# Cosine attention with a mixture of adapters on one core: sums of k and v of the last two batches kept head by head, and one tile multiplied in quarters of the array

## The chip, the cores and the metric

The kernel runs on one core of a Trainium2 chip. The metric is the time of one execution on the device, in microseconds (us). TensorE (PE; its weight loads are shown as PEld) multiplies matrices into PSUM. VectorE (DVE), ScalarE (ACT) and GpSimd (POOL) work element by element. SyncE (SP) and GpSimd issue the transfers (DMA) between HBM and the on-chip memory SBUF. Each engine runs its own list of instructions in order, and semaphores tell one engine that another has finished something.

## The reference

Linear attention with cosine weights over 8 batches of 8 heads, 576 positions and 64 dimensions, and then a mixture of eight low-rank adapters, two of them chosen for each of the 4608 rows:

```python
def phi(x, c, s):
    r = np.maximum(x, 0.0)
    return np.concatenate([r * c, r * s], axis=-1)
q_p, k_p = phi(q, cos_w, sin_w), phi(k, cos_w, sin_w)
kv = np.einsum('bhsf,bhsd->bhfd', k_p, v)
z = np.sum(k_p, axis=2)
num = np.einsum('bhsf,bhfd->bhsd', q_p, kv)
den = np.einsum('bhsf,bhf->bhs', q_p, z)[..., None] + 1e-06
x = (num / den).transpose(0, 2, 1, 3).reshape(B * S, H * D)
# then, with the two largest of the logits x @ w_gate for each row, w their softmax:
out = x + sum over the two e of  w_e * ((x @ A[e]) @ B[e])
```

## The kernel before

All matrix work is in bf16, with sums in PSUM. A table of text, `ORDER`, lists 791 steps, each with its engine letter (T TensorE, A ScalarE, V VectorE, G and W GpSimd, S SyncE) and its numbers; each engine's instructions stand in the order in which its steps stand there. There are two loops in it, interleaved: over the eight batches b, and over the 36 row tiles n of 128 rows (64 positions r times two values of s, of nine; every ninth tile, n = 4, 13, 22, 31, is mixed: one half of its rows is of one batch, the other of the next).

Steps of a batch: `ldv`, `ldk`, `ldq` load v, k and q (GpSimd issues, after the first batch). `vs` multiplies a ninth of v by a cosine or a sine; there are 18 for a batch, shared between ScalarE, GpSimd and in the first batches VectorE. `rk` and `qc` are the relu of k (one step) and of q (two steps), on VectorE (lines 251 and 282). `kv` (three parts, line 258) multiplies k and v into the PSUM tile `big`, in quarters of the array, heads by pairs. `kve` (line 275) copies that sum out of `big` into the SBUF tile `kvsb`, in bf16. `kvsb` has room for two heads side by side in its columns: the sums of heads with the first index half, g2 = 0, stand on partitions 0 to 63 in columns 0 to 64, those of g2 = 1 on partitions 64 to 127 in columns 65 to 129, with zeros elsewhere (written once by `kz`). So `kve` is two copies of 64 partitions, both on ScalarE, and the zeros let one matmul over all 128 rows give two heads without mixing them.

Steps of a tile: `qt` turns q on TensorE, `qe` multiplies it by the cosine and sine tables (VectorE, line 297, tile `qT`). `nd` multiplies it by `kvsb` into the PSUM tile `nd`, numerators and denominators together, after small matmuls that put the eps there. It has three forms: two heads at once with all 128 rows (tiles before 27); head by head with 64 rows (`by_rows`, from tile 27 on, lines 306 and 313); and for mixed tiles matmuls of 128 rows into 64 columns of the array for one batch and the other (lines 319 and 324). `re` (line 333) and `no` (lines 338 and 343) divide on VectorE and write the tile `xt`. `xt` turns it on TensorE, `xe` copies it (line 353), `za` (line 358) multiplies by the adapters' A and the gate. For groups of up to three tiles `mx`, `nm`, `mk`, `tt`, `cb`, `sg`, `zg`, `zt`, `ze` choose two adapters and weigh them. `dx` (lines 439 and 440) adds the tile and the adapters' part in a bank of `big`, which it shares with `kv`, `oe` copies it out (line 444), `st` stores it.

A step with the letter W is GpSimd's too, but waits besides for the latest VectorE step among `vs`, `rk`, `qc` that stands above it in the table. The program says so by a dependency that it calls "port".

## Time and profile before

| | |
|---|---|
| median of 3 runs | 106.73 us (106.12 to 106.85) |
| profiled execution | 105.92 us, span of the program 104.1 us |
| granted TensorE clock | 0.997 of full speed (2.4 GHz) |
| busy, TensorE / VectorE / ScalarE / GpSimd | 91.0 / 87.3 / 82.3 / 57.3 us |
| moved by DMA | 25.55 MB, mean 245 GB/s |

The span is counted from the first instruction of the program to the end of the last; the execution's time has some 1.8 us around it. Two stretches have a form of their own: up to about 26 us the first batches wait for their loads, and behind 94 us the last group's chain and the last stores run out. Between them the engines work all the time, each at its own list. An engine's busy time says how much of a stretch it worked; the chain of waits, followed back from the last instruction, names at each step who was waited for; the timeline gives each instruction with its start and its length.

### The profile page before, as it was taken

How to read it: one execution, taken by the hardware profiler on the slowest of the kernel's cores; microseconds unless marked ns; L12 is line 12 of the kernel's file. 1: busy time of each engine (PE TensorE's matmuls, PEld its weight loads, DVE VectorE, ACT ScalarE, POOL GpSimd, SP SyncE). 2: the span in 40 equal slices, each digit the busy share in tenths (PEclk: the TensorE clock that was granted, in tenths of full speed). 3: DMA queues.
4: the chain of work that ended last, by engine and by line, in shares of the span. 5: the costliest groups of instructions: out<-in, count | busy, mean ns of one | idle time of the engine just before them, and what ended most of it. 6: DMA issues, size and time to landing. Idle time of an engine off the chain costs nothing.

```text
span 104.1 us, 3984 instructions
## 1 busy us (share of the span) xinstructions
PE 91.0 (87%) x1620; PEld 65.7 (63%) x1620; DVE 87.3 (84%) x264; ACT 82.3 (79%) x176; POOL 57.3 (55%) x112
## 2 busy tenths in 40 slices
PE   4999489879794999999999999999999999998810
PEld 1344267457573887867887789688778677665200
DVE  5058769579995999999999999999999999999710
ACT  6969767918899699999899789979984896967820
POOL 6991004960799696997979869998910000000000
PEclk9999999999999999999999999999999999999998
DMA  2999999999999999999999999999999996989992
GB/s 27 364 358 291 216 208 247 208 207 213 203 208 213 204 206 210 208 213 204 208 210 205 208 207 207 210 206 126 188 397 372 349 334 257 376 307 383 381 384 96
DMA packets 19225, 25.55 MB, mean 245 GB/s; under 512 B 2184, under 2 KB 13448, under 8 KB 19208
## 3 DMA queue, kind: packets, MB, share of 16 engines
q0 software_dynamic: 11616, 12.98, 73.8%
q1 hardware_dynamic: 7064, 12.21, 32.8%
q8 instruction: 12, 0.20, 0.7%
q10 hardware_dynamic: 528, 0.13, 0.6%
q14 instruction: 5, 0.04, 0.1%
HBM read 28.85 MB, written 9.44 MB: 368 GB/s over the span
## 4 chain that ended last, share of the span: by engine, by line
PE 53%; DMA 18%; ACT 11%; POOL 9%; issue 2%; DVE 2%; POOLq 0%; ACTq 0%
DMA q<-in_q_dram 18%; PE nd L324 10%; PE big L258 8%; PE xz L349 6%; PE za L358 6%; PE big L439 6%; PE big L440 5%; PE pq L289 5%; POOL vs L244 4%; ACT xT L353 3%; ACT zgT L423 2%; PE nd L313 2%; POOL q L200 2%; PE xz L415 2%; POOL k L200 1%
## 5 line engine op out<-in xcount | busy, mean ns | idle before, releaser
L244 POOL TENSOR_SCALAR vs<-v,tab 128x256 bf16<-128x256 bf16 x78 | 37.9, 501 | 17.8 <-DMA v<-in_v_dram 8.7
L353 ACT COPY xT<-xz 128x512 bf16<-128x512 bf16 x34 | 20.0, 587 | 8.9 <-PE xz L349 8.3
L297 DVE TENSOR_TENSOR qT<-pq,tabq 128x1024 bf16<-128x1024 bf16 x36 | 23.8, 676 | 0.9 <-PE pq L289 0.8
L243 ACT ACTIVATE vs<-v,tab 128x256 bf16<-128x256 bf16 x43 | 20.0, 512 | 0.9 <-DMA v<-in_v_dram 0.6
L343 DVE TENSOR_TENSOR xt<-nd,rden 128x512 bf16<-128x512 f32 x28 | 19.2, 687 | 0.3
L324 PE MATMUL nd<-kvsb,qT 128*128 128x130 bf16 (+1 forms) x256 | 19.1, 221 | 0.4 <-DVE qT L297 0.4
L258 PE MATMUL big<-vs,k 64*64 64x130 bf16 x576 | 12.4, 221 | 4.3 <-DVE k L251 2.7
L324 PEld LDWEIGHTS <-qT 128*128 128x128 bf16 (+1 forms) x256 | 13.6, 100 | 2.9 <-issue 1.1
L349 PE MATMUL xz<-ident,xt 128*128 128x128 bf16 x144 | 14.1, 220 | 1.2 <-DVE xt L343 0.7
L358 PE MATMUL za<-AW,xT 128*128 128x136 bf16 x144 | 14.4, 223 | 0.1
L258 PEld LDWEIGHTS <-k 64*64 64x64 bf16 x576 | 9.2, 106 | 7.2 <-DVE k L251 3.5
L289 PE MATMUL pq<-ident,qq 128*128 128x128 bf16 x144 | 13.0, 219 | 0.2 <-DVE qq L282 0.2
L439 PE MATMUL big<-xt,turn 128*128 128x512 bf16 x31 | 11.7, 378 | 0.4 <-ACT k L444 0.3
L349 PEld LDWEIGHTS <-xt 128*128 128x128 bf16 x144 | 10.2, 114 | 2.6 <-DVE xt L343 0.9
L440 PE MATMUL big<-Ball,zgT 128*128 128x512 bf16 x31 | 11.8, 380 | 0.0
L468 PE MATMUL nd<-ones 128*128 128x512 bf16 x36 | 9.4, 427 | 1.5 <-DVE eps_hi L469 1.5
L275 ACT CAST kvsb<-big 64x520 bf16<-64x520 f32 x16 | 9.5, 593 | 1.5 <-PE big L258 1.1
L358 PEld LDWEIGHTS <-xT 128*128 128x128 bf16 x144 | 9.4, 98 | 1.9 <-ACT xT L353 0.8
L289 PEld LDWEIGHTS <-qq 128*128 128x128 bf16 x144 | 9.2, 98 | 1.9 <-DVE qq L282 0.3
L319 PE MATMUL nd<-eps_hi,ones 128*128 128x4 bf16 x56 | 9.5, 169 | 0.1
L282 DVE TENSOR_SCALAR qq<-q 128x1152 bf16<-128x1152 bf16 x16 | 8.1, 513 | 0.8 <-DMA q<-in_q_dram 0.8
L468 PEld LDWEIGHTS <-ones 128*128 128x128 bf16 x36 | 3.8, 108 | 6.6 <-issue 1.9
(81 smaller groups left out, 148.1 us busy)
## 6 DMA issues: line engine op xcount, KB each, us to landing
q<-in_q_dram POOLq DMA_DIRECT2D x8, 576.0 KB, 17.1
v<-in_v_dram POOLq DMA_DIRECT2D x7, 576.0 KB, 17.6
k<-in_k_dram POOLq DMA_DIRECT2D x7, 576.0 KB, 17.0
out_dram<-k SPq DMA_DIRECT2D x10, 256.0 KB, 4.2
out_dram<-v0f SPq DMA_DIRECT2D x8, 256.0 KB, 4.5
out_dram<-k0f SPq DMA_DIRECT2D x8, 256.0 KB, 3.8
out_dram<-v SPq DMA_DIRECT2D x6, 256.0 KB, 3.3
v0f<-in_v_dram SPq DMA_DIRECT2D x1, 1152.0 KB, 5.5
```

What stands on the lines that cost most here:

```text
L243: return e.activation(dst, src, AF.Copy, bias=0.0, scale=t)
L244: return e.tensor_scalar(out=dst, in0=src, scalar1=t, scalar2=1.0, op0=ALU.mult, op1=ALU.mult)
L258: e.matmul(out=big[halves[g2], par, gp * 2 * W:(gp + 1) * 2 * W], lhsT=k_b[b][pr, 2 * gp + g2, s, :], rhs=vs_t[b % NV][pr, s, 2 * gp + g2, ...
L289: e.transpose(out=d[:, gp, :, jj, :], in_=q2_t[b % 3][:, gp, s].rearrange("p g d -> p (g d)"), identity=ident)
L297: e.tensor_tensor(out=qT_t[n % NQ], in0=src, in1=tab, op=ALU.mult)
L324: e.matmul(out=nd[pr, par, gp * 2 * W:(gp + 1) * 2 * W], lhsT=qT[:, i, gp * 2 + par, js], rhs=kv_t[b % 3][:, par, gp, i, :], start=False, ...
L343: e.tensor_tensor(out=x.rearrange("p (a t d) -> p t a d", t=2, d=D), in0=nds()[:, :, :, 0:D], in1=rd.rearrange("p (t a) -> p t a", t=2).to ...
L349: e.transpose(out=xz[:, c * 128:(c + 1) * 128], in_=x[:, c], identity=ident)
L353: (e.copy if e is nc.scalar else e.tensor_copy)(xT_t[n % 3], src)
L358: e.matmul(out=zs[:, i, :], lhsT=xT_t[n % 3][:, c, :], rhs=AW[:, c, :], start=(c == 0 and i == 0), stop=(c == DCH - 1), skip_group_check=True)
L439: e.matmul(out=d, lhsT=turn, rhs=x_t[n % NX], start=True, stop=False)
L440: e.matmul(out=d, lhsT=zgT_t[g % 3][:, n - GROUPS[g][0], :], rhs=Ball, start=False, stop=True)
```

## The change

The sums of batches 6 and 7 (`dense(b)`) are no longer spread in `kvsb`: both halves go into columns 0 to 64, each on its own partitions, in one copy of 128 partitions by 520. The tiles from 27 on read them there; for `by_rows` tiles that is another column offset and nothing else. The mixed tile 31 has to be head by head then: 4 eps and 32 matmuls of 64 x 64 with 65 columns, in four quarters of the array, instead of 2 eps and 16 of 128 x 64 with 130 columns. Its division writes the same tile from another place in PSUM (`no`). `nm` gets a form for GpSimd.

```diff
-ROWS = 27
+ROWS, DENSE = 27, True
+def dense(b):
+    return DENSE and b >= ROWS // 9 * 2
     def kve(e, b, g2):
+        copy = e.copy if e is nc.scalar else e.tensor_copy
+        if dense(b):
+            return copy(kv_t[b % 3][:, :, :, :, 0:W], big[:, :, 0:4 * W].rearrange("p t (y i w) -> p t y i w", y=2, i=2))
...
     def nd_(e, n):
         qT, tok = qT_t[n % NQ], tokens(n)
+        if mixed(n) and dense(tok[0][0]):
+            jobs = [(g2, pr, js, kv_t[tok[j][0] % 3]) for g2, pr in enumerate(halves) for j, js in enumerate(halves)]
+            for g2, pr, js, _ in jobs:
+                e.matmul(out=nd[js, g2, D:4 * W:W], lhsT=ones[pr, 0:HALF], rhs=eps_hi2[pr], start=True,
+                         stop=False, skip_group_check=True)
+            for gp in range(2):
+                for par in range(2):
+                    for i in range(2):
+                        for g2, pr, js, kvb in jobs:
+                            a = gp * 2 + par
+                            e.matmul(out=nd[js, g2, a * W:(a + 1) * W], lhsT=qT[pr, i, a, js],
+                                     rhs=kvb[pr, par, gp, i, 0:W],
+                                     start=False, stop=(i == 1), skip_group_check=True)
+            return
         if by_rows(n):
-            kvb = kv_t[tok[0][0] % 3]
+            kvb, c = kv_t[tok[0][0] % 3], (0, 0 if dense(tok[0][0]) else W)
...
-                                     rhs=kvb[pr, par, gp, i, g2 * W:(g2 + 1) * W],
+                                     rhs=kvb[pr, par, gp, i, c[g2]:c[g2] + W],
...
     def no(e, n):
-        if by_rows(n):
+        if by_rows(n) or dense(tokens(n)[0][0]):
...
     def nm(e, g):
+        if e is nc.gpsimd:
+            m8 = m8_t[g % 2]
+            return e.tensor_tensor(out=ms_t[g % 2][:, 0:n], in0=m8[:, 0:n, 0], in1=m8[:, 0:n, 1], op=ALU.add)
...
-vs,G,4,5,0 vs,A,4,0,0 mx,V,10 mx,V,9 mx,V,11 nd,T,13 vs,G,4,3,0 nm,V,3 oe,A,6 rk,V,4,0 vs,W,4,2,1 oe,A,5 xt,T,12
+vs,A,4,3,1 dx,T,6,b1 vs,G,4,3,0 vs,A,4,0,0 mx,V,10 mx,V,9 mx,V,11 nd,T,13 vs,G,4,2,1 nm,V,3 oe,A,6 rk,V,4,0
+vs,W,4,1,1 oe,A,5 xt,T,12 qt,T,16 mk,V,3 re,V,13 qt,T,15 xe,A,12 tt,V,3 vs,G,4,7,0 no,V,13 dx,T,7,b1 vs,A,4,0,1
```

The table is written anew. The lists of TensorE, VectorE and SyncE have the same steps in the same order, `nm` still on VectorE. ScalarE's list loses `kve,A,6,1` and `kve,A,7,1`. GpSimd's list has the same steps in the same order too, but seven of its waits for VectorE stand one step later in the list (six letters W move, one step keeps its W and gets the next wait).

ScalarE at the sums of batch 6, before (`kvsb0` is the tile of the sums, `zgT0` the turned weights of a group, `vs1` v of batch 7):

```order
L353 COPY xT1_105<-xz_150 128x512 [waits PE_49,Activation_49]
L275 CAST kvsb0_88<-big_152 64x8x65 [waits PE_49]
L275 CAST kvsb0_88<-big_152 64x8x65
L423 COPY zgT0_120<-xz_150 128x3x2x64 [waits PE_49]
L243 ACTIVATE vs1_87<-v7_85,tab1_133 128x4x64
```

and of the change:

```order
L376 COPY xT1_105<-xz_150 128x512 [waits PE_49,Activation_49]
L279 CAST kvsb0_88<-big_152 128x8x65 [waits PE_49]
L449 COPY zgT0_120<-xz_150 128x3x2x64 [waits PE_49]
L248 ACTIVATE vs1_87<-v7_85,tab1_133 128x4x64
L248 ACTIVATE vs1_87<-v7_85,tab0_132 128x4x64
```

One copy of 128 partitions stands where two of 64 stood; the rest is as before.

GpSimd in batch 4, up to the load of q of batch 6 (`q1`), before (`vs0` is the scaled v; "waits DVE" is the wait of a W step, here for the relu of k of batch 4):

```order
L244 TENSOR_SCALAR vs0_86<-v4_82,tab0_132 128x4x64
L244 TENSOR_SCALAR vs0_86<-v4_82,tab1_133 128x4x64 [waits DVE_49]
L244 TENSOR_SCALAR vs0_86<-v4_82,tab1_133 128x4x64 [waits Pool_49]
L244 TENSOR_SCALAR vs0_86<-v4_82,tab0_132 128x4x64
L244 TENSOR_SCALAR vs0_86<-v4_82,tab1_133 128x4x64
L244 TENSOR_SCALAR vs0_86<-v4_82,tab0_132 128x4x64 x2
L244 TENSOR_SCALAR vs0_86<-v4_82,tab1_133 128x4x64 x2
L200 DMA q1_64<-in_q_dram 128x4x576 [waits DMASW3_49]
```

and of the change:

```order
L249 TENSOR_SCALAR vs0_86<-v4_82,tab0_132 128x4x64
L249 TENSOR_SCALAR vs0_86<-v4_82,tab1_133 128x4x64
L249 TENSOR_SCALAR vs0_86<-v4_82,tab1_133 128x4x64 [waits DVE_49,Pool_49]
L249 TENSOR_SCALAR vs0_86<-v4_82,tab0_132 128x4x64
L249 TENSOR_SCALAR vs0_86<-v4_82,tab1_133 128x4x64
L249 TENSOR_SCALAR vs0_86<-v4_82,tab0_132 128x4x64 x2
L249 TENSOR_SCALAR vs0_86<-v4_82,tab1_133 128x4x64 x2
L205 DMA q1_64<-in_q_dram 128x4x576 [waits DMASW3_49]
```

The wait for VectorE has gone one operation down.

GpSimd behind the load of k of batch 7 (`k7`), where the W steps of batch 5 and 6 wait for the relu of k and the second relu of q of batch 5, before:

```order
L200 DMA k7_78<-in_k_dram 128x4x576 [waits DMASW4_49]
L244 TENSOR_SCALAR vs1_87<-v5_83,tab0_132 128x4x64 [waits DVE_49,PE_49,Pool_49]
L244 TENSOR_SCALAR vs1_87<-v5_83,tab1_133 128x4x64 [waits DVE_49]
L244 TENSOR_SCALAR vs0_86<-v6_84,tab1_133 128x4x64 [waits DMASW0_49,PE_49,Pool_49]
L244 TENSOR_SCALAR vs0_86<-v6_84,tab1_133 128x4x64 [waits PE_49,Pool_49]
```

and of the change:

```order
L205 DMA k7_78<-in_k_dram 128x4x576 [waits DMASW4_49]
L249 TENSOR_SCALAR vs1_87<-v5_83,tab0_132 128x4x64 [waits PE_49,Pool_49]
L249 TENSOR_SCALAR vs1_87<-v5_83,tab1_133 128x4x64 [waits DVE_49]
L249 TENSOR_SCALAR vs0_86<-v6_84,tab1_133 128x4x64 [waits DVE_49,DMASW0_49,PE_49,Pool_49]
L249 TENSOR_SCALAR vs0_86<-v6_84,tab1_133 128x4x64 [waits PE_49,Pool_49]
```

Here the first operation behind the load has lost its wait for VectorE; the second waits for what the first waited for, and the third for what the second waited for. The other four are of the same kind: the waits for the two relus of batch 6's q, which stand behind the load of batch 7's q, and those for the relu of k of batches 6 and 7.

## Rows read from the trace of the kernel before

**Rows 1.** The page, part 1: busy us (share of the span) xinstructions.
```profile
PE 91.0 (87%) x1620; PEld 65.7 (63%) x1620; DVE 87.3 (84%) x264; ACT 82.3 (79%) x176; POOL 57.3 (55%) x112
```

**Rows 2.** Chain of waits, in order of time: start us, us, what.
```profile
70.91 0.49 ACT kvsb L275
71.42 0.59 ACT kvsb L275
```

**Rows 3.** Stretches: us, then busy us (xinstructions) by engine, clock, DMA share, GB/s.
```profile
70.00:78.00 8.00, 7.87 (x156) 6.25 (x153) 8.00 (x24) 7.36 (x17) 5.49 (x10) 1.00 1.05 234
78.00:86.00 8.00, 8.00 (x188) 5.97 (x181) 7.92 (x24) 5.92 (x12) 0.00 (x0) 1.00 0.96 353
86.00:94.00 8.00, 7.92 (x142) 5.55 (x142) 7.48 (x28) 6.00 (x13) 0.00 (x0) 1.00 0.85 315
```

**Rows 4.** Groups by line and form: busy us, mean ns of one, idle before.
```profile
L353 ACT COPY xT<-xz 128x512 bf16<-128x512 bf16 x34 | 20.0, 587 | 8.9 <-PE xz L349 8.3
...
L275 ACT CAST kvsb<-big 64x520 bf16<-64x520 f32 x16 | 9.5, 593 | 1.5 <-PE big L258 1.1
```

**Rows 5.** Timeline of weight loads at kv, batch 7: start us, us, what [idle before].
```profile
77.20 0.40 PEld L258 LDWEIGHTS <-k 64*64 64x64 bf16 x24 [0.27 <-issue]
```

**Rows 6.** Timeline of TensorE, 79 to 86 us: start us, us, what.
```profile
79.05 0.54 PE L258 MATMUL big<-vs,k 64*64 64x130 bf16 x24
79.52 0.18 PE L306 MATMUL nd<-eps_hi,ones 64*128 64x4 bf16 x2
...
79.90 0.41 PE L358 MATMUL za<-AW,xT 128*128 128x136 bf16 x4
...
83.00 0.38 PE L440 MATMUL big<-Ball,zgT 128*128 128x512 bf16 x1
83.31 0.18 PE L306 MATMUL nd<-eps_hi,ones 64*128 64x4 bf16 x2
...
84.76 0.38 PE L440 MATMUL big<-Ball,zgT 128*128 128x512 bf16 x1
84.98 0.17 PE L319 MATMUL nd<-eps_hi,ones 128*128 128x4 bf16 x1
...
85.90 0.41 PE L358 MATMUL za<-AW,xT 128*128 128x136 bf16 x4
```

**Rows 7.** Timeline of VectorE around tile 31.
```profile
84.72 1.27 DVE L297 TENSOR_TENSOR qT<-pq,tabq 128x1024 bf16<-128x1024 bf16 x2
86.01 0.21 DVE L333 RECIPROCAL rden<-nd 128x8 f32<-128x8 f32 x1
...
87.62 0.21 DVE L333 RECIPROCAL rden<-nd 128x8 f32<-128x8 f32 x1
```

**Rows 8.** Timelines of VectorE and of GpSimd at relus of k (lines 251, 244).
```profile
46.89 0.93 DVE L251 TENSOR_SCALAR k<-k 128x2304 bf16<-128x2304 bf16 x1
...
59.78 0.74 DVE L251 TENSOR_SCALAR k<-k 128x2304 bf16<-128x2304 bf16 x1
...
73.28 0.96 DVE L251 TENSOR_SCALAR k<-k 128x2304 bf16<-128x2304 bf16 x1
...
47.91 0.48 POOL L244 TENSOR_SCALAR vs<-v,tab 128x256 bf16<-128x256 bf16 x1 [0.71 <-DVE mk L380]
...
73.60 0.97 POOL L244 TENSOR_SCALAR vs<-v,tab 128x256 bf16<-128x256 bf16 x1
```

**Rows 9.** Timelines of VectorE and of GpSimd at relus of q (lines 282, 200).
```profile
51.46 0.45 DVE L282 TENSOR_SCALAR qq<-q 128x1152 bf16<-128x1152 bf16 x1
...
52.00 0.55 DVE L282 TENSOR_SCALAR qq<-q 128x1152 bf16<-128x1152 bf16 x1
...
70.17 0.79 DVE L282 TENSOR_SCALAR qq<-q 128x1152 bf16<-128x1152 bf16 x1
...
51.50 0.79 POOL L200 DMA_DIRECT2D q<-in_q_dram  x1
...
69.91 0.79 POOL L200 DMA_DIRECT2D q<-in_q_dram  x1
```

More of the change, by code (lines that the diff above doesn't have):

```diff
@@ L38 @@
+vs,G,2,4,0 qt,T,8 rk,V,2,0 nd,T,6 oe,A,0 ldq,G,4,0 xt,T,5 oe,A,1 qe,V,8 za,T,4 vs,W,2,1,1 xe,A,5 re,V,6
+vs,G,2,3,1 mx,V,4 vs,A,2,3,0 kv,T,2,0 no,V,6 ldv,G,5,0 vs,A,2,7,1 za,T,5 qc,V,2,1 vs,A,2,4,1 nd,T,7 mx,V,5
+qc,V,2,0 vs,A,2,8,1 xt,T,6 mk,V,1 kv,T,2,1 nm,V,1 re,V,7 xe,A,6 tt,V,1 cb,V,1 no,V,7 kv,T,2,2 sg,A,1 qt,T,9
 zg,V,1 kve,A,2,0 nd,T,8 vs,W,3,0,1 qe,V,9 kve,A,2,1 vs,G,3,0,0 xt,T,7 zt,T,1 qt,T,10 vs,G,3,5,0 re,V,8 za,T,6
[L39 removed]
@@ new lines @@
+vs,G,3,8,1 vs,A,3,2,0 za,T,7 re,V,9 dx,T,3,b1 ldq,G,5,0 xe,A,8 mx,V,7 no,V,9 dx,T,4,b0 vs,A,3,1,0 vs,G,3,6,1
+za,T,8 rk,V,3,0 nd,T,10 oe,A,4 vs,W,3,4,1 oe,A,3 xt,T,9 qt,T,12 mx,V,6 mx,V,8 re,V,10 vs,A,3,3,0 vs,G,3,3,1
+nm,V,2 kv,T,3,0 mk,V,2 no,V,10 vs,A,3,4,0 vs,G,3,7,0 xe,A,9 qe,V,12 vs,G,3,8,0 nd,T,11 vs,A,3,7,1 ldk,G,5,0
+tt,V,2 qc,V,3,1 kv,T,3,1 vs,A,3,6,0 re,V,11 xt,T,10 cb,V,2 ldv,G,6,0 qc,V,3,0 sg,A,2 kv,T,3,2 no,V,11 xe,A,10
+qt,T,13 ldk,G,6,0 kve,A,3,1 qt,T,14 zg,V,2 nd,T,12 vs,A,4,1,0 qe,V,14 vs,W,4,6,1 xt,T,11 kve,A,3,0 zt,T,2
@@ new lines @@
+xe,A,25 zg,V,7 nd,T,27 st,S,20 qc,V,7,1 zt,T,7 re,V,27 za,T,24 st,S,12 no,V,27 xt,T,26 za,T,25 st,S,11 xe,A,26
+kv,T,7,1 qc,V,7,0 nd,T,28 ze,A,7 mx,V,25 mx,V,24 st,S,16 qe,V,29 za,T,26 xt,T,27 st,S,15 re,V,28 kv,T,7,2
+mx,V,26 no,V,28 xe,A,27 st,S,4 qt,T,31 kve,A,7,0 nm,V,8 mk,V,8 nd,T,29 qe,V,30 st,S,9 xt,T,28 tt,V,8 re,V,29
+qt,T,32 cb,V,8 no,V,29 dx,T,21,b0 sg,A,8 xe,A,28 dx,T,22,b1 zg,V,8 nd,T,30 qe,V,31 oe,A,21 zt,T,8 xt,T,29
+oe,A,22 re,V,30 za,T,27 st,S,21 no,V,30 qt,T,33 xe,A,29 dx,T,23,b0 mx,V,27 ze,A,8 qe,V,32 nd,T,31 oe,A,23
@@ L85 @@
+zg,V,10 xt,T,34 nd,T,35 oe,A,27 st,S,26 xe,V,34 za,T,33 oe,A,29 re,V,35 zt,T,10 no,V,35 za,T,34 ze,A,10 st,S,29
+mx,V,33 mx,V,34 xt,T,35 nm,V,11 st,S,28 mk,V,11 dx,T,31,q1 tt,V,11 cb,V,11 dx,T,30,q0 st,S,27 xe,V,35 sg,A,11
+oe,A,31 dx,T,32,b0 zg,V,11 oe,V,30 za,T,35 oe,A,32 zt,T,11 st,S,31 mx,V,35 ze,A,11 mk,V,12 nm,V,12 zm,V,12
+st,S,32 dx,T,33,b1 sg,A,12 zg,V,12 st,S,30 dx,T,34,q1 oe,A,33 zt,T,12 oe,V,34 ze,A,12 st,S,33 dx,T,35,q0 st,S,34
+oe,A,35 st,S,35
 """
@@ L271, in kve @@
     def kve(e, b, g2):
+        copy = e.copy if e is nc.scalar else e.tensor_copy
+        if dense(b):
+            return copy(kv_t[b % 3][:, :, :, :, 0:W], big[:, :, 0:4 * W].rearrange("p t (y i w) -> p t y i w", y=2, i=2))
         src = big[halves[g2], :, 0:4 * W].rearrange("p t (y i w) -> p t y i w", y=2, i=2)
         dst = kv_t[b % 3][halves[g2], :, :, :, g2 * W:(g2 + 1) * W]
-        (e.copy if e is nc.scalar else e.tensor_copy)(dst, src)
+        copy(dst, src)
     def qc(e, b, h):
```

79 lines of the change are left out of this document (30 added, 49 removed).

## The prediction

> **What bounds the kernel now.** I read the page's busy times first. TensorE 91.0, VectorE 87.3 and ScalarE 82.3 us of a 104.1 us span [rows 1]: three engines near the limit, so the average does not tell which one sets the end. Next the chain of waits, in order of time. It ends with ScalarE's last copy out of PSUM, behind which only the last store remains. Going back it is mostly TensorE, but around 71 us it runs on ScalarE, and the two `kvsb` copies of batch 6 stand in it one behind the other, at 70.91 and 71.42 us [rows 2]. Read alone, this says that a copy less is 0.59 us less.
>
> The busy time by stretch says otherwise. From 70 to 78 us, the very stretch in which the chain is on ScalarE, VectorE is busy for 8.00 of 8.00 us; from 78 to 86 us for 7.92 of 8.00; only from 86 to 94 us does it have half a microsecond free [rows 3]. TensorE looks just as full, but its ends are modelled and include the drain of its pipeline, whereas VectorE's operations stand back to back with the time that they always take (two `qT` products in 1.27 us [rows 7]). A chain of waits names one of several engines that are equally late. The reader is to see that the order of VectorE's work is not touched by the change, so from 70 to 94 us the most that any relief of ScalarE and TensorE can bring is VectorE's idle time there: 24.00 - 8.00 - 7.92 - 7.48 = 0.60 us.
>
> **The change, part by part.**
>
> *One copy instead of two for batches 6 and 7 (ScalarE).* A copy of 64 partitions x 520 takes 593 ns; one of 128 partitions x 512 takes 587 ns [rows 4]. Partitions cost nothing here, so the merged copy is costed at 593 ns and two of four go: 2 x 0.59 = 1.19 us of ScalarE. In batch 6 the next ScalarE work could move up by 0.59 us, but what the chain comes to behind it is kv of batch 7, which TensorE begins at 77.20 us after standing still for 0.27 us [rows 5]. So TensorE gets at most 0.27 us, and the numerator block behind kv hands its result to VectorE, which is busy to the brim until 78 [rows 3]: nothing of it arrives at the end by itself. In batch 7, near 81.5 us, the same, with VectorE at 7.92 of 8.00. If VectorE had been idle there, 0.27 us would have been gained at the first place and up to 0.59 at the second.
>
> *Tile 31 in quarters (TensorE).* Before, the block of 2 eps and 16 matmuls of 128x64 with 130 columns takes from 84.98 to 85.90 us, 0.92 us [rows 6]. Now it is 4 eps and 32 matmuls of 64x64 with 65 columns, 8 rounds of four. The trace has no such form, so I bound it. Rounds of four with 130 columns: kv does six in 0.47 us (79.05 to 79.52), so eight take at most 0.63; the eps may add 0.04. Eight rounds of 65 columns in halves of the array, eps included: 0.38 us (79.52 to 79.90) [rows 6]. For going from the whole array to parts, a matmul of the whole array is followed only after 0.31 us by the eps of the next tile (83.00 to 83.31), where 0.22 us is what its 512 columns take otherwise (84.76 to 84.98): 0.09 us [rows 6]. So 0.47 to 0.76 us, a gain of 0.16 to 0.45 us on TensorE; I take the middle, 0.3.
> The Trainium skill has a rule against the lower end: "TensorEngine Tiling (Array Packing)", Gotcha 2, says that column tiling excludes the fast weight load, and "TensorE: Matmul & The Clock Gate", LDWEIGHTS, gives about P/1.2 ns for a load of P columns, an estimate of 53 ns a round and of about 0.6 us for the block. No row shows quarters with 65 columns. By it the block's gain would be 0.3 us instead of 0.45.
> Either way the block's result is wanted by VectorE's reciprocal at 86.01 us, and VectorE comes to it from two `qT` products that end at 85.99 [rows 7]: 0.02 us of the gain passes directly. What TensorE's lead (0.27 and 0.3 us) can still fill is VectorE's idle time behind it, such as the wait before the reciprocal at 87.62 [rows 7]. Much of the 0.60 us idle is one VectorE operation waiting for the result of another, which no lead removes. I take 0.15 us gained, 0 and 0.6 as bounds.
>
> *The normalising product of tile 31* has another stride pattern and the same size. *The new branch in `nm`* is for GpSimd, and `nm` stands on VectorE alone. Both are costed at nothing: VectorE has no operation more or less.
>
> *GpSimd's waits.* GpSimd's sequence is the same, but in seven places the wait for a VectorE operation sits one operation later. These VectorE operations (relu of k, relu of q) and GpSimd's hold each other up. The prices [rows 8]: a relu of k takes 0.74 us when left alone (59.78). The one at 73.28 started while a GpSimd operation was running and took 0.96, so 0.22 too long. The GpSimd operation behind it (73.60) stretched to 0.97 us and ended 0.33 us after the relu. An operation that waits by mark starts 0.09 us after the relu's end and needs 0.48 (47.91, after the relu of 46.89 that took 0.93), so it ends 0.57 us after. Unmarked is thus 0.24 us faster for GpSimd. A descriptor job for a load counts as well: the relu of q at 70.17, started 0.26 us into the job of 69.91, took 0.79 us, against 0.45 for the one at 51.46, which started just ahead of the job of 51.50 [rows 9]. That is 0.34 too long, so a relu is let through some 0.60 us after a job's start.
> The Trainium skill, "SBUF — State Buffer", section "Who interferes with whom", describes this as an exclusive lock on a port pair that VectorE and GpSimd share, held for the whole instruction. The trace agrees: 0.97 us for an operation of GpSimd that otherwise takes 0.48.
> Now the places, with these prices. (a) Batch 4: behind the relu of 46.89 GpSimd gains 0.24 us, so the job of 51.50 starts at 51.26 and the relu of q of 51.46 falls into it: held until 51.86, +0.40. The relu at 52.00, 0.10 us too long before (0.55 [rows 9]), then escapes: -0.10. (b) Batch 5: an operation now unmarked runs right behind the relu of 59.78 and is in the way of the next relu: about the 0.22 of 73.28. (c) Batch 7: the job of 69.91 hardly moves, but VectorE comes 0.3 to 0.5 us later, so its relu meets the end of the job and gets its 0.34 us back. (d) The operation unmarked behind that job ends earlier by the 0.24 us of an unmarked one and more, so the next one is running when the next relu comes: +0.15, an estimate below the 0.22 of 73.28. The relu of 73.28 as before. Sum: 0.40 - 0.10 + 0.22 - 0.34 + 0.15 = +0.33 us for VectorE. These are phases of tenths of a microsecond, and what VectorE loses before 70 us it partly makes up where it waits for TensorE; I take +0.1. The bounds are -0.6 (the relus of 70.17 and 73.28 both go free, 0.34 + 0.22, and nothing is lost) and +0.8 (a, b and d, and c is held as before: 0.30 + 0.22 + 0.15, with 0.1 more at 73.28).
>
> **The sum.** Nothing from ScalarE, -0.15 from TensorE's lead, +0.1 from GpSimd: about -0.1 us. The profiled execution took 105.92 us (span 104.1 and 1.8 around it), so 105.8 for one like it; it lies 0.8 us below the median of the runs shown, 106.73, and against that I forecast **106.6**.
>
> **The rivals.**
> *The saved work reaches the end.* If ScalarE's stretch sets the pace after all, 0.59 us in batch 6, as much in batch 7 and 0.3 us of tile 31 come off: 106.73 - 1.5 = 105.2. For it: the chain of waits [rows 2]. Against it: VectorE's 8.00 of 8.00 us in the same stretch [rows 3], with no operation less. Chance 0.12.
> *Slower: GpSimd in VectorE's way.* Its place is the descriptor job for batch 6's q, its first price 0.40 us; it decides as soon as the job starts 0.05 to 0.55 us ahead of the relu of 51.46, since every later meeting of the two engines is then shifted. By the upper bound above VectorE loses 0.8 us: 107.5. To pass one per cent it needs 0.3 us more, one further relu that meets a fresh operation. For it: each price stands in its row [rows 8, 9]. Against it: the meeting at 70.17 works the other way, and no single delay is over 0.4 us. Chance 0.10.
> *The quarters don't run four at a time.* If they go in pairs, 16 rounds at the rate of the eight in 0.38 us, the block takes 0.76 + 0.09 = 0.85 us, still not above the present 0.92, and the end is 106.7. This lies inside the forecast and has no chance of its own.
>
> **How the numbers follow.** Forecast (VectorE keeps the pace, the phases nearly cancel): 0.78, with an own range of 105.9 to 107.3, from the bounds of GpSimd's term and the spread of the runs before (106.12 to 106.85). Leaving out the far ends of both rivals, 105.6 to 107.5 holds 8 in 10. One per cent, 1.07 us, is about what a measurement of this kernel can tell from no change. Faster than 105.66 takes the first rival, 0.12; slower than 107.80 takes the second and its further relu, 0.07; the rest, 0.81, lies between.
>
> **What would show it.** In the changed profile: two `kvsb` copies of 128 partitions at about 0.59 us; VectorE busy for 7.9 us or more in each of the two stretches from 70 to 86 us; the block of tile 31 at 0.47 to 0.76 us; its reciprocal starting when the second `qT` product ends, not when the block ends; the relu of q near 51.5 us at about 0.85 us and the one near 70.5 at about 0.45. The forecast would be wrong if VectorE were idle for more than 0.6 us between 70 and 94 us, or if the time moved by more than VectorE's last tile product does.

## The result, and the profile after

The kernel became slower: 107.52 us (median of 20 runs, 106.82 to 108.2) against 106.27 us for the kernel before (20 runs, 105.62 to 107.89), a ratio of 1.0121 with a 95% interval of 1.0096 to 1.0145. The forecast was 106.6 us with a range up to 107.5, and a chance of 0.07 for more than one per cent slower. So the prediction was wrong: it forecast a small gain, and a loss clear of the noise came. Some executions fall into a slower state, whatever the kernel; the ratios leave them out, the medians and ranges count all. The profiled execution took 107.36 us, its span is 105.6 us against 104.1 before, 1.5 us more.

**The engines did nearly what was forecast.** The page, part 1, of the changed kernel (busy us, share of the span, instructions):

```profile
PE 90.5 (86%) x1625; PEld 65.7 (62%) x1638; DVE 87.1 (82%) x264; ACT 81.2 (77%) x174; POOL 58.6 (56%) x112
```

Against [rows 1], TensorE is busy 0.5 us less, ScalarE 1.1 us less, VectorE the same. ScalarE's two copies of the sums, on its timeline (start us, us, what):

```profile
71.28 0.61 ACT L279 CAST kvsb<-big 128x520 bf16<-128x520 f32 x1
...
81.23 0.61 ACT L279 CAST kvsb<-big 128x520 bf16<-128x520 f32 x1
```

One takes 0.61 us, where [rows 4] have 0.59 for half the partitions. The stretches that answer to [rows 3] (us, then busy us by engine, clock, DMA share, GB/s):

```profile
70.00:78.00 8.00, 7.91 (x157) 6.51 (x157) 8.00 (x24) 7.37 (x17) 5.70 (x10) 1.00 1.06 236
78.00:86.00 8.00, 7.95 (x222) 6.16 (x217) 7.93 (x25) 5.35 (x11) 0.00 (x0) 1.00 0.97 360
86.00:94.00 8.00, 7.35 (x136) 5.28 (x136) 7.60 (x29) 6.14 (x13) 0.00 (x0) 1.00 0.78 287
```

VectorE, the third engine of a row, is as full as before: 8.00, 7.93 and 7.60 us. The chain that ended last, which the prediction took for one of several equally late, has moved in large part to VectorE; its shares of the span, before and after:

```profile
PE 53%; DMA 18%; ACT 11%; POOL 9%; issue 2%; DVE 2%; POOLq 0%; ACTq 0%
```

```profile
DVE 31%; PE 28%; DMA 18%; POOL 9%; ACT 6%; issue 2%; POOLq 0%; ACTq 0%
```

TensorE around tile 31, which answers to [rows 6], and VectorE, which answers to [rows 7]:

```profile
85.00 0.20 PE L314 MATMUL nd<-eps_hi,ones 64*64 64x4 bf16 x4
85.05 0.42 PE L321 MATMUL nd<-kvsb,qT 64*64 64x65 bf16 x32
85.41 0.41 PE L381 MATMUL za<-AW,xT 128*128 128x136 bf16 x4
```

```profile
84.76 0.17 DVE L387 MAX8 m<-za 128x8 f32<-128x8 f32 x1
84.84 1.27 DVE L305 TENSOR_TENSOR qT<-pq,tabq 128x1024 bf16<-128x1024 bf16 x2
86.02 0.20 DVE L356 RECIPROCAL rden<-nd 128x8 f32<-128x8 f32 x1
...
87.48 0.21 DVE L356 RECIPROCAL rden<-nd 128x8 f32<-128x8 f32 x1
```

The block goes from 85.00 to 85.41, where the next product starts: 0.41 us instead of 0.92 (an expectation below counts to the end of its last row, 85.47, and says 0.47). The reciprocal behind it starts at 86.02 us, at 86.01 before. That is a gain, because VectorE came to it 0.12 us later (the `qT` products start at 84.84 against 84.72). VectorE's rows overlap by some 0.08 us where it waits for nothing (the products start at 84.84, the row before ends at 84.93). After, the reciprocal starts like that, 0.09 us before the products' row ends at 86.11; before, it started 0.02 us behind their end, so it waited some 0.1 us for the block, and this wait is gone. The next reciprocal comes 0.14 us earlier (87.48 against 87.62). This lead lasts to the end of the compute: ScalarE's last copy of the output, before and after, on its timelines:

```profile
99.38 0.58 ACT L444 COPY v<-pq 128x512 f32<-128x512 f32 x1 [0.48 <-PE pq L440]
```

```profile
99.22 0.58 ACT L470 COPY v<-pq 128x512 f32<-128x512 f32 x1 [0.48 <-PE pq L466]
```

In these two traces all computing is over 0.16 us **earlier** than before, and the span ends 1.5 us **later**. What lies between is the stores. (The lead is no more than traces of one kernel differ: in a second trace of the changed kernel, further down, this copy starts at 99.52 us.)

**Where the time went.** SyncE's list of stores, first before, then after (start us, us, what; each store is 256 KB, "x4" groups four that follow each other):

```profile
93.86 2.52 SPq L451 DMA_DIRECT2D out_dram<-k0f  x4
96.48 2.67 SPq L451 DMA_DIRECT2D out_dram<-k  x4
99.24 1.28 SPq L451 DMA_DIRECT2D out_dram<-v  x2
```

```profile
94.25 2.53 SPq L477 DMA_DIRECT2D out_dram<-k0f  x4
96.88 3.43 SPq L477 DMA_DIRECT2D out_dram<-k  x4
100.40 1.21 SPq L477 DMA_DIRECT2D out_dram<-v  x2
```

Before, the last two stores are issued by 99.24 + 1.28 = 100.52 us, as soon as the last copy is done at 99.96; after, by 101.61, though the last copy is done at 99.80. That is 1.09 us. SyncE is 0.4 us late at 94 and 96 us already (four runs below without the loss are 0.2 to 0.4 us late there too), and the four stores from 96.88 take 3.43 instead of 2.67 us. From the last issue to the end of the span it is 3.99 us (105.6 - 101.61) against 3.58: 0.41 us more, 1.5 in all. The DMA view from 95 to 101 us, in 40 slices of 0.15 us, before:

```profile
DMA  9999999999999999999999999999999999999999
...
q1 hardware_dynamic: 1264, 2.29, 102.5%
```

and after:

```profile
DMA  9999899999999999998999711139999999999999
...
q1 hardware_dynamic: 1123, 2.05, 92.3%
q8 instruction: 1, 0.02, 1.0%
```

Before, the 16 DMA engines are busy without a gap. After, they stand nearly still for four slices, 98.45 to 99.05 us ("1113"), and there is one packet of another queue in the stretch: q8, "instruction", 16 KB of TensorE's own code. The packet records of the trace put it at 96.99 us, 0.96 us long; the dip comes half a microsecond behind its end. What is long among the four stores is the one that SyncE starts beside the transfer: its issue takes 1.47 us, to 98.35, and right behind that comes the dip (SyncE's timeline, 96.8 to 97.3 us):

```profile
96.88 1.47 SPq L477 DMA_DIRECT2D out_dram<-k  x1
```

The page, part 3, counts this queue (packets, MB, share), before and after:

```profile
q8 instruction: 12, 0.20, 0.7%
```

```profile
q8 instruction: 13, 0.21, 0.8%
```

The change gives TensorE 36 instructions more (18 weight loads and 18 matmuls: 1638 weight loads instead of 1620 in the trace, as many matmuls; the page after lists 1625 of them, 13 records are missing), and its code needs a thirteenth transfer within the span, near the end, when the stores fill the DMA engines. The earlier ones are nothing new. In the kernel before, the last lay at 89.69 us, and the DMA view from 88 to 92 us, in slices of 0.1 us, shows the same dip behind it:

```profile
DMA  9999999999999999999999999999989961000079
```

and a store issued beside that transfer takes as long:

```profile
89.79 1.36 SPq L451 DMA_DIRECT2D out_dram<-v  x1
```

There SyncE has caught up with the compute by its last two stores (issued at 99.24 and as soon as the copy of 99.38 is done); behind a transfer at 97 us it has not. The Trainium skill, "Runtime: NRT & Kernel Launch", section "Instruction fetch mechanics", says that an engine's code comes in blocks of 16 KiB, 256 instructions, and that crossing into the next costs "one DMA tail-bump, mostly hidden". The size agrees with the trace (0.20 MB in 12 packets; that a block is 256 instructions no run here counts); hidden it was not here.

### The profile page after: what moved, and what is told of

Same layout as the page of the kernel before. It is cut to its first block, busy times and chain, and to the rows that moved or that the text cites. A ratio compares the mean times of both kernels' runs of the same rounds, so it can differ in the third digit from the quotient of the medians.

```text
span 105.6 us, 4007 instructions
## 1 busy us (share of the span) xinstructions
PE 90.5 (86%) x1625; PEld 65.7 (62%) x1638; DVE 87.1 (82%) x264; ACT 81.2 (77%) x174; POOL 58.6 (56%) x112
## 4 chain that ended last, share of the span: by engine, by line
DVE 31%; PE 28%; DMA 18%; POOL 9%; ACT 6%; issue 2%; POOLq 0%; ACTq 0%
DMA q<-in_q_dram 18%; DVE qT L305 9%; DVE xt L366 7%; PE nd L347 5%; DVE qq L290 5%; POOL vs L249 4%; PE xz L372 3%; DVE xt L361 3%; PE za L381 3%; PE big L465 3%; PE big L466 3%; PE big L263 3%; PE pq L297 2%; DVE rden L356 2%; PE xz L441 2%
## 5 line engine op out<-in xcount | busy, mean ns | idle before, releaser
L249 POOL TENSOR_SCALAR vs<-v,tab 128x256 bf16<-128x256 bf16 x78 | 39.0, 516 | 16.2 <-DMA v<-in_v_dram 8.5
L366 DVE TENSOR_TENSOR xt<-nd,rden 128x512 bf16<-128x512 f32 x27 | 18.6, 688 | 0.2
L347 PE MATMUL nd<-kvsb,qT 128*128 128x130 bf16 (+1 forms) x240 | 18.3, 221 | 0.4 <-DVE qT L305 0.4
L347 PEld LDWEIGHTS <-qT 128*128 128x128 bf16 (+1 forms) x240 | 13.1, 100 | 2.7 <-issue 1.0
L494 PE MATMUL nd<-ones 128*128 128x512 bf16 x36 | 10.8, 473 | 1.5 <-DVE eps_hi L495 1.5
L465 PE MATMUL big<-xt,turn 128*128 128x512 bf16 x28 | 10.6, 378 | 0.5 <-ACT k L470 0.3
L290 DVE TENSOR_SCALAR qq<-q 128x1152 bf16<-128x1152 bf16 x16 | 8.6, 543 | 0.8 <-DMA q<-in_q_dram 0.8
L466 PE MATMUL big<-Ball,zgT 128*128 128x512 bf16 x23 | 8.7, 380 | 0.2
L283 ACT CAST kvsb<-big 64x520 bf16<-64x520 f32 x12 | 7.1, 594 | 1.4 <-PE big L263 1.1
```

What stands on the lines that cost most here:

```text
L249: return e.tensor_scalar(out=dst, in0=src, scalar1=t, scalar2=1.0, op0=ALU.mult, op1=ALU.mult)
L290: return e.tensor_scalar(out=dst, in0=src, scalar1=0.0, scalar2=None, op0=ALU.max)
L347: e.matmul(out=nd[pr, par, gp * 2 * W:(gp + 1) * 2 * W], lhsT=qT[:, i, gp * 2 + par, js], rhs=kv_t[b % 3][:, par, gp, i, :], start=False, ...
L366: e.tensor_tensor(out=x.rearrange("p (a t d) -> p t a d", t=2, d=D), in0=nds()[:, :, :, 0:D], in1=rd.rearrange("p (t a) -> p t a", t=2).to ...
L494: nc.tensor.matmul(out=nd[:, 0, :], lhsT=ones[:, 0:128], rhs=ones, start=True, stop=True)
```

## The experiments

**Theory F**: the loss is the thirteenth code transfer, which holds up the stores of the tail. **Theory G**: it is GpSimd's shifted waits, as in the second rival of the prediction. Later runs met further rivals, named in their expectations. The medians are beside the runs of the kernel before on the same chip.

### Fewer TensorE instructions: 24 instead of 36 matmuls in the warm-up

```diff
-DUMMIES = 36
+DUMMIES = 24
```

> The changed kernel with 24 of the 36 warm-up multiplications at the start instead of all 36, so TensorE's list is 24 instructions shorter; all else as changed. Theory F: the changed kernel is slow because its 36 more TensorE instructions call for one more 16 KB transfer of instructions (the page's queue q8 has 13 packets in place of 12, the last at 96.99 us), which holds up the saturated stream of stores near the end. By F this list is short enough again: 12 packets on q8, no transfer behind 92 us, and the time comes back to 106.2 or less (before: 106.27 over 20 runs, changed: 107.52). Theory G (GpSimd's shifted waits cost VectorE its time): nothing of that is touched, so 107.5. A third way, that TensorE loses its clock without the 12 multiplications, would show as a lower granted clock before 20 us and a time above 107.5.

Measured: 106.59 us (10 runs, 105.89 to 107.67) against 106.28, ratio 1.0016 (0.9970 to 1.0062); F had said 106.2 or less. Twelve transfers in the span, the last at 88.60 us. SyncE's four stores are back to their old length:

```profile
96.73 2.53 SPq L477 DMA_DIRECT2D out_dram<-k  x4
```

The stretches from 8 us on show what the shorter warm-up cost at the start:

```profile
8.00:12.00 4.00, 0.63 (x3) 0.10 (x1) 2.67 (x7) 3.36 (x10) 0.28 (x1) 1.00 1.15 267
12.00:16.00 4.00, 3.13 (x80) 2.90 (x82) 1.97 (x6) 1.94 (x3) 0.00 (x0) 0.50 1.24 213
```

TensorE, busy 0.63 of 4 us, then got the clock at 0.50, its lower level of 1.2 GHz, from 12 to 16 us. By 34 us VectorE was ahead of the changed kernel again, by 0.4 us. F holds in what it said of the transfers and in that the loss goes, but this run changes two things at once; the last pair of runs below separates them.

### More TensorE instructions alone: the kernel before with 18 tiny matmuls, and with 4

```diff
+                for _ in range(18):
+                    nc.tensor.matmul(out=nd[:, 0, 0:4], lhsT=ones[:, 0:128], rhs=ones[:, 0:4], start=True, stop=True)
```

> The kernel before with 18 more multiplications of 4 columns behind the 36 warm-up ones (36 more TensorE instructions, some 1 us of TensorE near 11 us, where it waits for its first sums anyway); nothing else of the change. By F q8 has 13 packets, the last near 97 us, and the time rises from 106.27 to about 107.4. By G, or by any theory that puts the loss on copies, quarters or waits, it stays at 106.3.

Measured: 107.75 us (4 runs, 107.1 to 110.66), ratio 1.0120 (1.0016 to 1.0225). Nothing of the change is in this kernel except the number of TensorE's instructions, and a loss of the same size is there, though four runs give a wide interval. Thirteen transfers, the last at 97.61 us, and both marks of it:

```profile
96.79 3.48 SPq L451 DMA_DIRECT2D out_dram<-k  x4
```

```profile
DMA  9999999999999999998999999971113999999999
```

The same with `range(4)`:

> The kernel before with four matmuls of four columns more behind the warm-up (8 TensorE instructions with their weight loads, 0.1 us of work). F, with a block of 256 instructions per transfer: the thirteenth transfer of the changed kernel was asked for with about 16 to 20 instructions left of its 36 more, so 8 are too few to cross into a new block: twelve transfers, 106.2 to 106.5 us. Rival E (each further instruction costs, in proportion): 8/36 of 1.25 us, so 106.6; more matmuls in the warm-up disturb the start: 107 and more.

Measured: 106.34 us (10 runs, 105.81 to 107.82) against 106.26, ratio 1.0016 (0.9977 to 1.0055); twelve transfers, and

```profile
96.71 2.66 SPq L451 DMA_DIRECT2D out_dram<-k  x4
```

So 8 more cost nothing that can be measured, 36 more cost 1.2%. The times alone don't exclude a price per instruction (8/36 of 1.2% is 0.27%, inside the interval); that it is a step is read from the transfers, twelve with 8 more and thirteen with 36.

### The quarters alone

The kernel before, in which only tile 31 is multiplied in quarters, out of the spread sums:

```diff
+        if n == 31:
+            jobs = [(g2, pr, js, kv_t[tok[j][0] % 3]) for g2, pr in enumerate(halves) for j, js in enumerate(halves)]
...
```

> The kernel before with tile 31 alone multiplied in quarters (4 eps and 32 matmuls of 64x64 with 65 columns, read from the spread sums), two copies per batch and GpSimd's waits as before. By F it has the 36 instructions and so the 13th packet: about 107.4. By G: 106.3 or a little less, since the block itself is shorter (0.47 us in the changed kernel's timeline against 0.92).

Measured: 107.37 us (10 runs, 106.94 to 107.72), ratio 1.0098 (1.0061 to 1.0134), thirteen transfers, the last at 96.68 us, and

```profile
96.73 3.38 SPq L466 DMA_DIRECT2D out_dram<-k  x4
```

The quarters bring the 36 instructions and with them the loss, without the sums in one piece and without the new table.

### GpSimd's waits alone

The kernel before with only the seven waits moved, in the table:

```diff
-vs,G,4,5,0 vs,A,4,0,0 mx,V,10 mx,V,9 mx,V,11 nd,T,13 vs,G,4,3,0 nm,V,3 oe,A,6 rk,V,4,0 vs,W,4,2,1 oe,A,5 xt,T,12
+vs,A,4,3,1 dx,T,6,b1 vs,G,4,3,0 vs,A,4,0,0 mx,V,10 mx,V,9 mx,V,11 nd,T,13 vs,G,4,2,1 nm,V,3 oe,A,6 rk,V,4,0
+vs,W,4,1,1 oe,A,5 xt,T,12 qt,T,16 mk,V,3 re,V,13 qt,T,15 xe,A,12 tt,V,3 vs,G,4,7,0 no,V,13 dx,T,7,b1 vs,A,4,0,1
...
```

> The kernel before with the changed kernel's table, both copies of batches 6 and 7 put back, so that only GpSimd's seven waits are moved. By F: 12 packets on q8 and the time of before, 106.3 within 0.3. By G: up to the whole loss, 107.5. My own term for it was +0.1, with bounds -0.6 and +0.8.

Measured: 106.35 us (10 runs, 106.15 to 107.53), ratio 1.0018 (0.9979 to 1.0056), twelve transfers, and the four stores

```profile
96.85 2.75 SPq L451 DMA_DIRECT2D out_dram<-k  x4
```

G falls: the moved waits hold VectorE up where the prediction put it, and nothing measurable of it arrives at the end.

### Two attempts to take instructions away that told less

The changed kernel without the twelve matmuls between tiles whose results nobody reads:

```diff
-cw,A,0 qe,V,1 dm,T,n0 dm,T,n0 dm,T,n0 nd,T,0 qt,T,3 re,V,0 qt,T,2 no,V,0 qe,V,3 vs,G,1,8,0 vs,A,1,3,1 dm,T,b0
+cw,A,0 qe,V,1 nd,T,0 qt,T,3 re,V,0 qt,T,2 no,V,0 qe,V,3 vs,G,1,8,0 vs,A,1,3,1
...
```

> The changed kernel without the twelve 512-column matmuls between 14 and 26 us whose results nobody reads (24 TensorE instructions with their weight loads; the 36 of the warm-up stay). Theory F (a thirteenth 16 KB transfer of TensorE's code, at about 97 us, holds up the saturated stores): twelve transfers on the instruction queue, none after 90 us, stores landing every 0.64 us from 93 us to the end, 106.1 to 106.5 us, ratio to before 0.998 to 1.002; the granted clock may fall for some us between 14 and 26, which the run without twelve warm-up matmuls regained by 34 us. Rival D (the 1.2 us belong to the sums in the spread layout or to the quarters themselves, and the run with fewer warm-up matmuls gained it back by its lower clock elsewhere): 107.2 to 107.6.

Measured: 107.89 us (6 runs, 106.88 to 108.36), ratio 1.0141 (1.0082 to 1.0199): F's time was missed, rival D's was met and passed. The transfers are twelve, and the traced execution, the fastest of the six at 106.88 us, has the stores in order:

```profile
97.12 2.65 SPq L477 DMA_DIRECT2D out_dram<-k  x4
```

Its compute is late by itself (ScalarE's last copy starts at 99.84 us). The other five ran at a mean granted clock of 0.961 to 0.976, against 0.988 in the traced one, and took 107.28 to 108.36 us; none of them was traced, so what they lost and where stays open. The clock alone doesn't explain it: nine of the ten runs with the short warm-up had 0.951 to 0.973 and a median of 106.59 us in all ten. As a test of F this run is spoilt by what else it changed.

The changed kernel with 24 of the warm-up's matmuls replaced by 12 in fp32, meant to keep TensorE busy with fewer instructions:

```diff
+                for _ in range(12):
+                    nc.tensor.matmul(out=nd[:, 0, 0:256], lhsT=one32[:, 0:128], rhs=one32, start=True, stop=True)
-                for _ in range(DUMMIES):
+                for _ in range(DUMMIES - 24):
```

> The changed kernel with 24 of the 36 matmuls of the warm-up (bf16, 512 columns, each with a weight load) replaced by 12 of 256 fp32 columns, so that the program has 36 TensorE instructions fewer and TensorE should stay about as long busy. Theory F: twelve transfers on the instruction queue, none between 92 us and the end, no dip of the DMA row between 95 and 101 us; if the granted clock stays near 0.98 as in the changed kernel, 106.0 to 106.5 us, ratio to before 0.997 to 1.002. Should the chip run each fp32 matmul as several instructions, the thirteenth transfer stays, and F expects 107.3 to 107.7. Rival C (what the run without the twelve matmuls between tiles lost was no clock but belongs to the change): 107.3 to 107.9 with twelve transfers and an undisturbed clock.

Measured: 108.05 us (6 runs, 106.61 to 108.39), ratio 1.0102 (1.0024 to 1.0181). The page counts 1638 matmuls, 12 more than the program has (1638 - 24 + 12 = 1626): the trace lists 24 fp32 matmuls with 24 weight loads where the program has 12, so no instruction was saved. The thirteenth transfer stayed, at 97.31 us, with its hold-up:

```profile
97.59 3.28 SPq L478 DMA_DIRECT2D out_dram<-k  x4
```

This is the branch in which F expected 107.3 to 107.7, and the median lies above it. It tells against nothing and shows little.

### Slack for the stores

If the transfer costs only because the stores have no slack, leaving stores out should give the time back. First the three stores of tiles 17, 19 and 6 were left out of both kernels (the table of the kernel before):

```diff
-oe,A,23 qe,V,33 za,T,28 st,S,23 xt,T,30 re,V,31 za,T,29 no,V,31 st,S,17 xe,A,30 dx,T,24,b1 mx,V,29 mx,V,28
-st,S,19 nd,T,32 oe,A,24 nm,V,9 mk,V,9 qt,T,34 tt,V,9 st,S,6 re,V,32 xt,T,31 cb,V,9 no,V,32 dx,T,25,b0 sg,A,9
+oe,A,23 qe,V,33 za,T,28 st,S,23 xt,T,30 re,V,31 za,T,29 no,V,31 xe,A,30 dx,T,24,b1 mx,V,29 mx,V,28
+nd,T,32 oe,A,24 nm,V,9 mk,V,9 qt,T,34 tt,V,9 re,V,32 xt,T,31 cb,V,9 no,V,32 dx,T,25,b0 sg,A,9
```

> The changed kernel without the stores of tiles 17, 19 and 6 (768 KB not written, so three tiles of the output are missing), which stood at 86.5, 87.1 and 88.1 us in the row of stores. Three places of 0.64 us are 1.9 us of slack for the stores behind them, and the code transfer at 97 us takes 1.3 us of the stream. F: the thirteenth transfer is still there at 97 us, but the stream has caught up with the compute before it, so the time is that of the last tile's product and its own store: 105.7 to 106.2, and within 0.3 of the kernel before without the same stores. Rival H (the transfer holds up SyncE's queue or TensorE by itself, whatever the stream holds): 107.0 to 107.5.

> The kernel before without the stores of tiles 17, 19 and 6 (the same three tiles of the output missing). Its last store waits for the last copy of the output at 99.96 us, so the end of the compute stays: only the queue in front of the last store shrinks, 2.97 us from issue to landing. F: 105.7 to 106.2, a fall of 0.1 to 0.6. Rival (the stores alone set the time of before too): a fall of 1.2 to 1.9, 104.4 to 105.1.

Measured: the kernel before falls to 105.98 us (10 runs), ratio 0.9972 (0.9938 to 1.0007), as F expected: the fall of 1.2 to 1.9 us that stores alone would bring doesn't come, and the 0.3 us of the medians can't be told from none. The changed kernel does not fall: 107.8 us (4 runs, 106.77 to 108.22), ratio 1.0132 (1.0061 to 1.0203). F's expectation failed, and rival H's 107.0 or more was met. Its trace, of an execution of 108.22 us, shows two things that may be the reason. On TensorE's timeline, in the numerator block of a tile:

```profile
83.05 0.39 PE L336 MATMUL nd<-kvsb,qT 64*128 64x65 bf16 x14 [1.34 <-issue]
```

TensorE stood still for 1.34 us in the middle of a block, waiting for nothing that the profile shows; the code transfer that starts at 78.4 to 79.7 us in eleven of the fifteen traces started at 80.78 here. The copies of the output are late too, the last one by 1.48 us (100.70 against 99.22). And the stores that had been let off did not leave slack where the thirteenth transfer falls (97.96 us here): SyncE waits for compute until 95.6 us, and from there the last stores come one behind the other again.

So two stores of the tail itself were left out, those of tiles 31 and 32 (`st,S,31` and `st,S,32` out of the table), again from both:

> The changed kernel without the stores of tiles 31 and 32, which stood at 96.9 and 98.4 us in the row (512 KB, two tiles of the output missing): two places of 0.65 us, so that the hold-up of 1.3 us by the code transfer at 97 us meets as much slack in the stores themselves. F: the thirteenth transfer is still there, the time falls to 106.0 to 106.5, within 0.4 of the kernel before without the same two stores. Rival H (the transfer makes TensorE or SyncE late by itself, whatever the stores hold): 107.0 or more.

> The kernel before without the stores of tiles 31 and 32 (the same two tiles of the output missing). Its last store waits for the last copy of the output, so the time falls only by what the queue in front of the last store shrinks: 105.5 to 106.2 by F. Rival (the stores alone set its end): 104.8 to 105.1.

Measured: the kernel before 106.09 us (12 runs), ratio 0.9975 (0.9939 to 1.0011); the changed kernel 107.23 us (12 runs, 106.01 to 107.68), ratio 1.0055 (1.0016 to 1.0094). Between the two the change still costs 0.8% by the ratios; with some 0.4 points either way on each, this can't be told from the 1.21% of the change itself. F's expectation of 106.0 to 106.5 us failed again, and H's 107.0 or more was met. The trace again has TensorE standing still at 82 us,

```profile
82.38 0.39 PE L336 MATMUL nd<-kvsb,qT 64*128 64x65 bf16 x14 [0.76 <-issue]
```

against 0.30 us in that of the kernel before without these stores, and it still has the dip behind the transfer at 96.95 us. (The kernel before without these stores has its DMA engines idle from 98.95 to 100.00 us with no code transfer near: there no store is waiting.) So these two pairs do not show that the loss comes from the stores' want of slack. What they show is that a dip follows the transfer even where the stores have some room, and that TensorE, too, can stand still late in the kernel; how often it does in untraced executions is not known.

### The same number of instructions less, with the warm-up's end kept

The clean form of the first experiment: 24 matmuls instead of 36, begun later, so that they end when the 36 end.

```diff
-                for _ in range(DUMMIES):
-                    nc.tensor.matmul(out=nd[:, 0, :], lhsT=ones[:, 0:128], rhs=ones, start=True, stop=True)
...
+                if what == "tq":
+                    for _ in range(24):
+                        nc.tensor.matmul(out=nd[:, 0, :], lhsT=ones[:, 0:128], rhs=tabq[:, 1, 0:8, :], start=True, stop=True)
```

> The changed kernel with 24 instead of 36 matmuls in the warm-up, begun only when the table of the angles is written, at about 4.0 us instead of 1.5 (the first thirteen ran 0.43 us each and the rest 0.21, so 24 of them end at about 12 us, where the 36 end at 12.2): 24 TensorE instructions fewer and no idle TensorE between the warm-up and the first sums. F: twelve transfers on the instruction queue, none between 92 us and the end, no dip of the DMA row between 95 and 101 us, granted clock as in the changed kernel; 106.0 to 106.5 us, ratio to before 0.997 to 1.002, and at least 0.8 us below the changed kernel run beside it. Rival C (the loss sits in the sums in the spread layout or in the quarters): 107.2 to 107.6, the same as the changed kernel beside it.

> The changed kernel itself, beside the one above and the kernel before on the same chip, with a second trace. F: thirteen transfers, the last at about 97 us, a dip of the DMA row behind it, 107.2 to 107.8 us, 1.0096 to 1.0145 times before as measured first. Theory S (TensorE also waits for its code near 82 us, 0.3 to 1.3 us in six traces so far, and more with the new order of stores and waits): this trace shows such a wait, and the time lies above 107.5.

Measured, both on one chip: 106.53 us (12 runs, 105.81 to 107.59), ratio 1.0022 (0.9993 to 1.0052), for the one; 107.29 us (6 runs, 107.06 to 108.03), ratio 1.0109 (1.0076 to 1.0143), for the changed kernel itself. The intervals do not touch. F's bounds (106.5 us, 1.002, 0.8 us below) are missed by a hair, with 0.76 us between the two medians. The row of 24 in the warm-up, the four stores and the DMA view from 95 to 101 us of the first:

```profile
4.05 7.11 PE L515 MATMUL nd<-tabq,ones 128*128 128x512 bf16 x24 [4.05 <-ACT tabq L242]
```

```profile
96.81 2.56 SPq L477 DMA_DIRECT2D out_dram<-k  x4
```

```profile
DMA  9999999999999999999999999998999899999999
```

TensorE is busy from 4.05 to 11.16 us, the granted clock is 1.00 in each stretch from 8 to 40 us as in the changed kernel, there are twelve transfers in the span, none between 89.38 us and its end, and no dip. All of the change is in this kernel, sums, quarters and waits; without the 24 instructions its loss is gone. Rival C falls.

The thirteenth transfer is not gone, though: it now comes at 106.37 us, behind the end of the span at 104.6, where the page doesn't count it. The DMA view of this run from 104 to 108 us has

```profile
q8 instruction: 1, 0.02, 2.3%
```

(the same at 105.81 and 105.90 us in the two other runs with 24 instructions less; the kernel before has none there, and with 8 instructions more it has none either, while these three have 12 more). The traced execution is the longest of the twelve, 107.59 us, and 3.0 us of that lie outside its span; in the twelve it is 1.7 to 3.0 us, in those of the kernel before beside them 1.7 to 1.8. So the spans are the same (medians of 104.3 and 104.4 us), and the 0.35 us by which the medians differ lie outside. That the transfer behind the end costs them isn't shown: in the two runs of the kernel before with stores left out 1.8 to 2.2 us lie outside as well, and their traces have no such transfer.

The changed kernel's second trace repeats the first: thirteen transfers, the last at 96.92 us, 3.09 us for the four stores, and a dip

```profile
DMA  9999999999999999999999999610499999999999
```

TensorE's wait near 82 us is 0.17 us in it. The traced execution is the longest of the six, 108.03 us, as theory S would have it; but the median is 107.29, and the first trace of the changed kernel has the loss without any such wait, so S isn't needed for the loss.

Put together, by the length of the four stores from about 97 us: with twelve transfers 2.53 to 2.75 us (the kernel before, fewer warm-up matmuls, 8 instructions more, the waits alone, the late warm-up, no matmuls between tiles); with thirteen 3.09 to 3.48 (the change twice, 36 instructions more, the quarters alone, the fp32 warm-up). The version with the late warm-up takes the loss away and gains nothing measurable over the kernel before; no version with its whole output beats it.

## Why the prediction was wrong

**The step that failed** is "Tile 31 in quarters". It says what the change issues, "4 eps and 32 matmuls of 64x64" for "2 eps and 16", and prices them by their time on TensorE alone. The 18 more matmuls and their 18 weight loads are also code, and code is transferred. What was missing is a term for it: about +1.4 us (the forecast was -0.1, the medians moved by +1.25; by the traces, the last copy by -0.16 and the span by +1.5). That the 36 instructions bring this loss is shown: they do it by themselves and as the quarters alone, and taking 24 away ends it. That it runs through the thirteenth transfer and the stores beside it is read from the traces of these runs. The page had the row, "q8 instruction: 12, 0.20, 0.7%"; read as a share of the DMA engines it looks like nothing, and so it was not read at all. The dip behind the transfer at 89.69 us stood in the trace of the kernel before.

**Behind it stands a second sentence**, in "What bounds the kernel now": the chain ends with ScalarE's last copy, "behind which only the last store remains". That holds before, and only just: the stores follow the compute at the rate that the DMA engines take them, with about 0.2 us to spare (2.67 and 1.28 us for the last four and two, where stores back to back take 2.53 and 1.21). The tail was taken as a constant behind the compute and was never costed as a stage with a limit of its own. That the want of slack there makes the transfer dear is not shown: with two of the tail's stores left out the change still cost 0.8%. One of the two signs that the prediction named did show it: the time moved by more, and the other way, than VectorE's last products did. The other did not: VectorE was idle for 0.47 us from 70 to 94 us (24.00 - 8.00 - 7.93 - 7.60), less than the 0.6 that it asked for.

**ScalarE's copies: right.** Nothing of the 1.19 us that were saved arrived; VectorE is as full as before, and TensorE's gap before kv of batch 7 only shrank (0.18 us instead of the 0.27 of [rows 5]):

```profile
77.33 0.40 PEld L263 LDWEIGHTS <-k 64*64 64x64 bf16 x24 [0.18 <-issue]
```

The first rival, the saved work reaching the end, did not come.

**The block of tile 31: a little better than the bounds.** 0.41 us, where 0.47 to 0.76 was given; so the third rival, quarters that go in pairs at 0.85 us, is out. The lower bound took quarters with 65 columns to be no faster than halves; and the estimate of 0.6 us by the rule of the Trainium skill ("TensorE: Matmul & The Clock Gate", LDWEIGHTS) was too long. The reciprocal started with the end of the `qT` products, as said, but "0.02 us of the gain passes directly" misread the rows: VectorE had been waiting some 0.1 us for the block. That and the 0.14 us at the next reciprocal came through, some 0.25 us where the sum had 0.15.

**GpSimd's waits: right in kind, off in one place and so in the sum.** VectorE's relus of q, answering to [rows 9]:

```profile
51.40 0.87 DVE L290 TENSOR_SCALAR qq<-q 128x1152 bf16<-128x1152 bf16 x1
...
52.31 0.40 DVE L290 TENSOR_SCALAR qq<-q 128x1152 bf16<-128x1152 bf16 x1
...
60.39 1.11 DVE L290 TENSOR_SCALAR qq<-q 128x1152 bf16<-128x1152 bf16 x1
...
70.64 0.41 DVE L290 TENSOR_SCALAR qq<-q 128x1152 bf16<-128x1152 bf16 x1
...
71.57 0.60 DVE L290 TENSOR_SCALAR qq<-q 128x1152 bf16<-128x1152 bf16 x1
```

(a) was +0.40 and -0.10 for the first two: 0.87 against 0.45 is +0.42, 0.40 against 0.55 is -0.15. (c) was -0.34 for the one at 70.64: 0.41 against 0.79, -0.38. (d) was +0.15 for the next: 0.60 against 0.45, +0.15. (b) was +0.22, and this was too small: the relu at 60.39 took 1.11 us against 0.44, +0.67, since GpSimd came with two operations there and not with one. So these relus lost 0.71 us where the sum had 0.33; most of that VectorE made up where it waits. The relu of 73.28 had 0.94 us against 0.96. At 84.8 us VectorE is 0.12 us late, close to the +0.1 of the sum, and the waits alone measured 1.0018 (0.9979 to 1.0056), or +0.2 us with an interval that holds the +0.1 of the sum. The second rival named a loss, but by another mechanism; that the time ended near its 107.5 is chance.

**The range** ended at 107.5 and the time came at 107.52, but the reasons for the bounds had nothing to do with what happened. It came so near only because the forecast started from the 106.73 us of three runs; from the 106.27 of the twenty, -0.1 us is 106.17, and the miss is 1.35 us and not 0.92.

## What to carry to other kernels

Count the instructions that an edit adds to an engine's program, not only their time: each block of code is a transfer of its own, and the row for the instruction queue in the DMA part of the page says how many there are. Where the end of a kernel is a row of stores at the rate of the DMA engines, look whether a code transfer falls into it, and move that transfer behind the last store by taking out idle filler instructions ahead of it rather than by undoing the edit. Here 24 were enough. And a tail of stores is a stage: read its slack (SyncE's rows against the last copies) before taking it as a constant behind the compute.
